# Loading K of one head pair and V of the pair before it with one transfer of rows twice as long

## The chip, the cores and the metric

The kernel runs on one core of one Trainium2 chip. The metric is the device time of one execution in microseconds (us). The kernel before took 520.97 us (median of 4 runs, 520.58 to 522.02).

## The reference

One token passes through two identical layers: attention over the last 4,096 positions of a key and value cache, 32 heads of 192, then a gated MLP. There is one query, so each K and V element is used once per layer and the work is moving data. wq and wo are the weights that make the query and that turn the heads' outputs into the result.

```python
def _A_ref(x, k_cache, v_cache, wq, wo):          # D = 640, Hq = Hkv = 32, Dh = 192, W = 4096
    q = (x @ wq).reshape(...)                     # [1, 32, 1, 192]
    k = k_cache[:, :, Sk - W:, :]; v = v_cache[:, :, Sk - W:, :]
    p = softmax(einsum("bhqd,bhkd->bhqk", q, k) * Dh ** -0.5)
    return einsum("bhqk,bhkd->bhqd", p, v).reshape(...) @ wo
x = x + _A_ref(layernorm(x), ...); x = x + _B_ref(layernorm(x), ...)   # MLP, F = 1536
x = x + _A_ref(layernorm(x), ...); x = x + _B_ref(layernorm(x), ...)   # the same weights and caches again
```

## The kernel before

Heads go in 16 pairs. A pair has two units of 14,208 bf16 elements per partition: an A unit (wq and K) and a B unit (V and wo). On-chip memory holds seven slots of one unit and an area for the MLP weights. Every unit is one transfer of 128 rows of 28,416 B, from two arrays in memory. A slot is loaded again when its last reader is done. What fits is kept for layer 1 (pairs 0, 14, 15 and K of pair 1).

```python
def slot(s, o, n):
    return big[:, s * UNIT + o:s * UNIT + o + n]
A_SLOT = [{p: p % 2 for p in range(NPAIR)}, {p: 5 if p % 2 else 2 for p in range(NPAIR)}]
B_SLOT = [{p: 2 + p % 2 for p in range(NPAIR)}, {p: 3 if p % 2 else 6 for p in range(NPAIR)}]
# ... exceptions at the ends cut
# order of loads: a0, a1, b0, a2, b1, a3, b2, ...; the last V of a layer in three pieces (b1, b0, b0)
if k in ("a", "b"):
    s = (A_SLOT if k == "a" else B_SLOT)[it[1]][it[2]]
    if not take(s):
        return False                              # its slot is still in use
    pg.dma(q_dma(slot(s, 0, n), (ua if k == "a" else ub)[it[2]][:, 0:n]), f"s{s}", wr=[rslot[s]])

def step(p, prev):                                # one pair; p's scores, prev's values
    if l == 0 and prev > 0:
        PVn(prev - 1, 1 - prev % 2)               # times wo; releases the B slot of prev - 1
    Q(p, 0); QK(p, 0)                             # query, scores; releases the A slot of p
    soft(); expo()
    PVmm(prev, prev % 2)                          # weights times V
    ET(p % 2); PVt(prev % 2)
    if l == 1:
        PVn(prev, prev % 2)
```

`PVn`, the product with wo, is the last reader of a B slot.

## Time and profile before

The first view is the page of the kernel before, cut to the engines' busy times (PE is the matrix engine, PEld its weight loads, DVE VectorE, ACT ScalarE, POOL GpSimd), the 40 equal slices of the span with the DMA engines' busy tenths and their GB/s, and the table of DMA queues.

```profile
span 520.6 us, 8422 instructions
PE 272.0 (52%) x3716; PEld 139.7 (27%) x3716; DVE 98.0 (19%) x372; ACT 87.6 (17%) x171; POOL 2.0 (0%) x5
...
DMA  8999999999999999999999999999999999999996
GB/s 352 427 439 427 433 430 430 432 430 430 434 430 429 432 434 426 437 430 425 430 414 382 371 437 434 429 427 436 429 424 439 430 426 434 432 424 434 423 424 273
DMA packets 11835, 219.45 MB, mean 422 GB/s; under 512 B 1448, under 2 KB 1448, under 8 KB 4264
...
q1 hardware_dynamic: 11672, 219.13, 98.9%
q8 instruction: 13, 0.21, 0.2%
```

The queue of loads keeps the 16 DMA engines busy for 98.9% of the span, while the matrix engine is busy for 52%. The rate is flat at about 430 GB/s but for the start, the end and three slices at the layer boundary (382 and 371 among them).

The waits view of the same kernel (engine, tile and line, who released it: us in total, times, longest) shows the matrix engine waiting for both kinds of load.

```profile
PE bank L351 <- DMA big<-in_ua_dram: 71.1, 22, 4.1
...
PE o L420 <- DMA big<-in_ub_dram: 52.3, 26, 2.5
```

The timeline shows one pair in the steady loop (start us, us, engine, line and operation, and in brackets the idle time before it and what ended that; SPq is the queue that issues the loads).

```profile
140.78 0.56 PE L351 MATMUL bank<-sh,big 128*128 128x1 bf16 x15 [3.10 <-DMA big<-in_ua_dram]
141.69 2.75 PE L366 MATMUL scores<-big,qs 128*32 128x512 bf16 x24 [0.35 <-DVE qs L354]
144.48 0.33 SPq L182 DMA_DIRECT2D big<-in_ua_dram  x1
...
149.20 2.73 PE L420 MATMUL o<-big,et_sb 128*2 128x384 bf16 x32 [2.20 <-DMA big<-in_ub_dram]
...
153.99 0.56 PE L450 MATMUL bank<-sh,big 128*128 128x1 bf16 x15 [0.55 <-DVE sh L439]
154.58 0.33 SPq L182 DMA_DIRECT2D big<-in_ub_dram  x1
```

K lands (140.78), the scores are made, K's slot is loaded again (144.48); V lands (149.20), wo is applied, V's slot is loaded again (154.58). These loads land about 30 us after their issue, so in the steady loop about two and a half loads are queued ahead of each:

```profile
big<-in_ua_dram SPq DMA_DIRECT2D x27, 3552.0 KB, 30.0
big<-in_ub_dram SPq DMA_DIRECT2D x24, 3552.0 KB, 28.3
```

(That is the list of DMA issues: what, how many, KB each, median us from issue to landing.) The trace also has a record for each row that an engine moved. Their median durations, of the kernel before:

```
row, bytes   3,840   7,680   15,360   16,384   24,576   28,416
median, ns     149     292      575      611      912     1,055
```

### The profile page before, as it was taken

Reading aid. Unit: us, or ns where it says so; the run is one execution under the profiler, and the core shown is the slowest. Engines: PE = TensorE matmul, PEld = TensorE weight load, DVE = VectorE, ACT = ScalarE, POOL = GpSimd, SP = SyncE. Lnnn points to the kernel's source line nnn. Section 1 sums busy time; section 2 is a strip of 40 time slices with the busy share of each in tenths; the row PEclk is TensorE's granted clock in tenths of the full one; section 3 lists DMA queues with packets and bytes.
Section 4 is the critical chain, followed back from the end, with each engine's and each line's share of the span. In section 5 each row is a group of like instructions: output and inputs, shape, how many; then the busy total and the mean of one; then the engine's idle time right before and its main releaser. Section 6 shows DMA issues by size and latency. Waiting matters only on the chain. (4 is left out here: it accounts for less than half of the span.)

```text
span 520.6 us, 8422 instructions
## 1 busy us (share of the span) xinstructions
PE 272.0 (52%) x3716; PEld 139.7 (27%) x3716; DVE 98.0 (19%) x372; ACT 87.6 (17%) x171; POOL 2.0 (0%) x5
## 2 busy tenths in 40 slices
PE   0645354545445453645465667866354545455465
PEld 0322122212222222222224434433122212222234
DVE  0222111111111201211121233322111211121211
ACT  0112102210121112210120023132102211121110
POOL 0010000000000000000000000000000000000000
PEclk9999766556555555555565559776555555556655
DMA  8999999999999999999999999999999999999996
GB/s 352 427 439 427 433 430 430 432 430 430 434 430 429 432 434 426 437 430 425 430 414 382 371 437 434 429 427 436 429 424 439 430 426 434 432 424 434 423 424 273
DMA packets 11835, 219.45 MB, mean 422 GB/s; under 512 B 1448, under 2 KB 1448, under 8 KB 4264
## 3 DMA queue, kind: packets, MB, share of 16 engines
q1 hardware_dynamic: 11672, 219.13, 98.9%
q8 instruction: 13, 0.21, 0.2%
q10 hardware_dynamic: 144, 0.06, 0.0%
q14 instruction: 6, 0.05, 0.0%
HBM read 219.18 MB, written 0.00 MB: 421 GB/s over the span
## 5 line engine op out<-in xcount | busy, mean ns | idle before, releaser
L420 PE MATMUL o<-big,et_sb 128*2 128x384 bf16 x1024 | 81.7, 488 | 52.3 <-DMA big<-in_ub_dram 52.3
L366 PE MATMUL scores<-big,qs 128*32 128x512 bf16 x744 | 82.5, 611 | 9.9 <-DVE qs L354 9.8
L379 ACT ACTIVATE diag<-cst,sc 128x128 f32<-128x128 bf16 x32 | 12.8, 401 | 265.7 <-DVE sc L376 258.8
L351 PE MATMUL bank<-sh,big 128*128 128x1 bf16 x480 | 17.5, 166 | 72.0 <-DMA big<-in_ua_dram 71.1
L376 DVE TENSOR_REDUCE sc<-scores 128x1 f32<-128x1024 f32 x31 | 38.0, 1224 | 80.3 <-PE scores L366 80.3
L420 PEld LDWEIGHTS o<-big,et_sb 128*2 128x2 bf16 x1024 | 28.0, 109 | 92.9 <-DMA big<-in_ub_dram 60.9
L382 PE MATMUL bank<-diag,sc 128*128 128x128 f32 x64 | 23.3, 463 | 48.4 <-ACT diag L379 48.4
L390 ACT ACTIVATE e_sb<-scores,sc 128x1024 bf16<-128x1024 f32 x31 | 37.3, 1205 | 41.7 <-DVE sc L385 39.8
L425 ACT CAST o_sb<-o 128x384 bf16<-128x384 f32 x64 | 30.3, 477 | 70.7 <-PE o L420 70.6
L351 PEld LDWEIGHTS bank<-sh,big 128*128 128x128 bf16 x480 | 15.7, 105 | 74.9 <-DMA big<-in_ua_dram 72.9
L366 PEld LDWEIGHTS scores<-big,qs 128*32 128x32 bf16 x744 | 23.9, 132 | 44.0 <-issue 30.7
L382 PEld LDWEIGHTS bank<-diag,sc 128*128 128x128 f32 x64 | 14.6, 285 | 73.8 <-ACT diag L379 72.3
L400 DVE CAST et_sb<-bank 128x64 bf16<-128x64 f32 x32 | 7.2, 225 | 122.4 <-PE bank L396 122.4
L354 DVE TENSOR_TENSOR qs<-bank,cst 128x96 bf16<-128x96 f32 x32 | 8.2, 258 | 103.5 <-PE bank L351 103.2
L450 PE MATMUL bank<-sh,big 128*128 128x1 bf16 x480 | 17.6, 166 | 15.8 <-DVE sh L439 15.6
L403 PE MATMUL bank<-sc 128*128 128x2 f32 x64 | 16.5, 328 | 14.5 <-DVE sc L401 14.5
L450 PEld LDWEIGHTS bank<-sh,big 128*128 128x128 bf16 x480 | 14.9, 102 | 18.3 <-DVE sh L439 17.3
L403 PEld LDWEIGHTS bank<-sc 128*128 128x128 f32 x64 | 13.8, 268 | 17.3 <-DVE sc L401 17.3
L383 DVE TENSOR_REDUCE sc<-bank 128x2 f32<-128x128 f32 x32 | 9.3, 292 | 42.3 <-PE bank L382 42.3
L396 PEld LDWEIGHTS bank<-cst,e_sb 128*128 128x128 bf16 x256 | 9.1, 104 | 22.9 <-ACT o_sb L425 16.5
L396 PE MATMUL bank<-cst,e_sb 128*128 128x8 bf16 x256 | 11.9, 170 | 5.6 <-ACT e_sb L390 5.6
L405 DVE RECIPROCAL sc<-bank 64x1 f32<-64x1 f32 x64 | 10.6, 166 | 20.5 <-PE bank L403 19.5
(61 smaller groups left out, 101.3 us busy)
## 6 DMA issues: line engine op xcount, KB each, us to landing
big<-in_ua_dram SPq DMA_DIRECT2D x27, 3552.0 KB, 30.0
big<-in_ub_dram SPq DMA_DIRECT2D x24, 3552.0 KB, 28.3
big<-in_ub_dram SPq DMA_DIRECT2D x2, 3072.0 KB, 27.0
big<-in_ub_dram SPq DMA_DIRECT2D x4, 768.0 KB, 17.4
big<-in_wd_dram SPq DMA_DIRECT2D x3, 960.0 KB, 7.6
big<-in_ua_dram SPq DMA_DIRECT2D x1, 2048.0 KB, 13.1
big<-in_ub_dram SPq DMA_DIRECT2D x1, 2016.0 KB, 16.3
big<-in_ub_dram SPq DMA_DIRECT2D x4, 480.0 KB, 18.0
```

Of the source, the lines that this page charges most:

```text
L351: ins = t.matmul(qe[:, i:i + 1], lhsT=slot(sa, c * 2 * DH + c0, P), rhs=xq[:, c:c + 1], start=(c == 0), stop=(c == DC - 1))
L366: ins = t.matmul(sc_x[1 + b][32 * j:32 * j + 32, :], lhsT=qs[:, y, k, :], rhs=slot(sa, WQE + k * W + (4 * b + j) * 512, 512), start=(k == ...
L376: pg.op("dve", lambda v: v.reduce_max(out=mx, in_=sc_x[0][:], axis=AX.X), wr=[res("mx")], ex=sc_x[3:5])
L379: pg.op("act", lambda a: a.mul(out=diag[:], in_=ident, mul=mx), rd=[res("cst"), res("mx")], wr=[res("diag")])
L382: pg.op("pe", lambda t: t.matmul(dmx[:, 0:P], lhsT=ones_f, rhs=diag[:], start=True, stop=True), rd=[res("diag"), res("ones")], ex=[rb[2]])
L390: pg.op("act", lambda a: a.activation(out=e_sb[:], in_=sc_x[0][:], func=ACT.Exp, bias=nbias, scale=srs_c, accum_out=rowsum), rd=[res("nbia ...
L396: ins = t.matmul(qe[:, 0:2 * NB].rearrange("p (r x) -> p r x", r=2)[:, :, 4 * b:4 * b + 4], lhsT=e_sb[:, b * P:(b + 1) * P], rhs=sel, star ...
L403: pg.op("pe", lambda t: t.matmul(dmx[:, P:P + 2], lhsT=ones_f, rhs=rs2, start=True, stop=True), rd=[res("rs2"), res("ones")], ex=[rb[2]])
L405: pg.op("dve", lambda v, h=h: v.reciprocal(out=Rn[z][64 * h:64 * h + 64], in_=dmx[64 * h:64 * h + 64, P + h:P + h + 1]), wr=[res(f"Rn{z}{h ...
L420: ins = t.matmul(o8[h][32 * j:32 * j + 2, 0:2 * DH].rearrange("p (a d) -> p a d", a=2), lhsT=et_sb[:, z, h * NB + 2 * u:h * NB + 2 * u + 2 ...
L425: pg.op("act", lambda a, h=h: a.copy(out=o8_sb[:, :, h * DH:(h + 1) * DH], in_=o8[h][:, 0:2 * DH].rearrange("p (a d) -> p a d", a=2)), wr= ...
L450: ins = t.matmul(yT[:, j:j + 1], lhsT=wo[:, c * D + j * P:c * D + (j + 1) * P], rhs=oTb[z][:, c:c + 1], start=False, stop=(c == 2), skip_g ...
```

## The change

The intent is fewer and longer rows. In memory, the A unit of pair p now lies beside the B unit of pair p - 1, and so do their slots on chip (which of the two comes first alternates with p). A new item "c" loads both with one transfer of 128 rows of 56,832 B. The two slots are filled together, and only when both are free. V's arrival is passed on through a one-element GpSimd memset, so that the matrix engine can wait for one count whether V came jointly or alone. The loads around the layer boundary and at the end of layer 1 stay separate, and so do K of pair 6 and V of pair 5 in layer 1. V and wo of pair 0, two loads before, come with the first joint one, and GpSimd's copy of that wo now runs early.

```diff
+    PLACE = {s: i for i, s in enumerate((0, 3, 2, 1, 4, 5, 6))}
     def slot(s, o, n):
-        return big[:, s * UNIT + o:s * UNIT + o + n]
+        return big[:, PLACE[s] * UNIT + o:PLACE[s] * UNIT + o + n]
...
-    A_SLOT = [{p: p % 2 for p in range(NPAIR)}, {p: 5 if p % 2 else 2 for p in range(NPAIR)}]
-    B_SLOT = [{p: 2 + p % 2 for p in range(NPAIR)}, {p: 3 if p % 2 else 6 for p in range(NPAIR)}]
+    A_SLOT = [{p: p % 2 for p in range(NPAIR)}, {p: 6 if p % 2 else 3 for p in range(NPAIR)}]
+    B_SLOT = [{p: 2 + p % 2 for p in range(NPAIR)}, {p: 2 if p % 2 else 5 for p in range(NPAIR)}]
...
+    seq = [("a", 0, 0)] + [("c", 0, p) for p in range(1, 15)] + [("a", 0, 15), ("b", 0, 14)] + last_values(0, 15)
+    seq += [("wol", 14), ("wol", 15)] + [(k,) for k in (*MW, *MV)] + [("wom",), ("a0", 0), ("a0", 1), ("a", 1, 3), ("b", 1, 2)]
+    seq += [("c", 1, p) for p in range(4, 13)] + [("a", 1, 13), ("b", 1, 12)] + last_values(1, 13)
     seq += [("fg",), ("fu",), ("fd", 0), ("fd", 1), ("fd", 2)]
+    seq = [y for x in seq for y in ([("a", *x[1:]), ("b", x[1], x[2] - 1)] if x in (('c', 1, 6),) else [x])]
...
+    def values_in(s):
+        pg.op("pool", lambda g: g.memset(tick, 0.0), rd=[rslot[s], res("tick")], wr=[rval[s], res("tick")])
...
+        if k == "c":
+            l, p = it[1:]
+            ss = A_SLOT[l][p], B_SLOT[l][p - 1]
+            if any(x in busy for x in ss):
+                return False
+            busy.update(ss)
+            first = min(ss, key=PLACE.get)
+            pg.dma(q_dma(slot(first, 0, 2 * UNIT), uc[p]), f"c{l}{p % 2}", wr=[rslot[x] for x in ss])
+            values_in(ss[1])
```

More of the change, by code (lines that the diff above doesn't have):

```diff
@@ L105, in decode_kernel @@
 @with_exitstack
-def decode_kernel(ctx: ExitStack, nc, cx: bass.AP, ua: bass.AP, ub: bass.AP,
+def decode_kernel(ctx: ExitStack, nc, cx: bass.AP, uc: bass.AP,
                   wg_d: bass.AP, wu_d: bass.AP, wd_d: bass.AP, out: bass.AP):
@@ L125, in decode_kernel @@
     et_sb = sb("et_sb", [P, 2, 2 * NB], BF16)
-    sc = sb("sc", [P, 24 + 5 * DC + 2 * FC], FP32)
+    sc = sb("sc", [P, 25 + 5 * DC + 2 * FC], FP32)
+    tick = sc[0:1, 24 + 5 * DC + 2 * FC:25 + 5 * DC + 2 * FC]
     mx, nbias, rowsum, rs_c, ss_c, lnv_c, srs_c, rstd_c, eps_a, eps_m, ones_c, Rn_0, Rn_1 = (sc[:, i:i + 1] for i in range(13))
@@ L166, in decode_kernel @@
     rslot = [res(f"slot{i}") for i in range(NSLOT)]
+    rval = [res(f"val{i}") for i in range(NSLOT)]
     rc = [res(f"cell{i}") for i in range(-(-ME // FW))]
@@ L171, in decode_kernel, with v_at, wo_at, a_in @@
     VAFTER = {"v0": "up2", "v1": "up1", "v2": "down0", "v3": "down1"}
+    PLACE = {s: i for i, s in enumerate((0, 3, 2, 1, 4, 5, 6))}
     def slot(s, o, n):
-        return big[:, s * UNIT + o:s * UNIT + o + n]
+        return big[:, PLACE[s] * UNIT + o:PLACE[s] * UNIT + o + n]
+    def v_at(p):
+        return 0 if p % 2 else WOE
+    def wo_at(p):
+        return VE if p % 2 else 0
+    def a_in(p, o0=0, o1=UNIT):
+        o = UNIT if p % 2 else 0
+        return uc[p][:, o + o0:o + o1]
+    def b_in(p, o0=0, o1=UNIT):
+        o = UNIT if p % 2 else 0
+        return uc[p + 1][:, o + o0:o + o1]
     def mreg(o, n):
@@ L193, in decode_kernel, with last_values @@
     NHALF = NB * DH // 2
-    def stream(l, ps):
-        q = list(ps)
-        out_ = []
-        for i, p in enumerate(q):
-            out_.append(("a", l, p))
-            if i:
-                out_.append(("b", l, q[i - 1]))
-        return out_ + [("b1", l, q[-1]), ("b0", l, q[-1], 0), ("b0", l, q[-1], 1)]
-    seq = stream(0, range(NPAIR))
-    seq.insert(seq.index(("b", 0, 0)) + 1, ("wo0",))
-    seq += [("wol", 14), ("wol", 15)] + [(k,) for k in (*MW, *MV)]
-    tail = stream(1, range(2, 14))
-    assert tail[0] == ("a", 1, 2)
-    seq += [("wom",), ("a0", 0), ("a0", 1)] + tail[1:]
+    def last_values(l, p):
+        return [("b1", l, p), ("b0", l, p, 0), ("b0", l, p, 1)]
+    seq = [("a", 0, 0)] + [("c", 0, p) for p in range(1, 15)] + [("a", 0, 15), ("b", 0, 14)] + last_values(0, 15)
+    seq += [("wol", 14), ("wol", 15)] + [(k,) for k in (*MW, *MV)] + [("wom",), ("a0", 0), ("a0", 1), ("a", 1, 3), ("b", 1, 2)]
+    seq += [("c", 1, p) for p in range(4, 13)] + [("a", 1, 13), ("b", 1, 12)] + last_values(1, 13)
     seq += [("fg",), ("fu",), ("fd", 0), ("fd", 1), ("fd", 2)]
+    seq = [y for x in seq for y in ([("a", *x[1:]), ("b", x[1], x[2] - 1)] if x in (('c', 1, 6),) else [x])]
     seq_pos = [0]
-    busy = {2}
+    busy = set()
     ev_done = {}
@@ L223, in take @@
         return True
+    def values_in(s):
+        pg.op("pool", lambda g: g.memset(tick, 0.0), rd=[rslot[s], res("tick")], wr=[rval[s], res("tick")])
     def try_load(it):
         k = it[0]
-        if k in ("a", "b"):
-            s = (A_SLOT if k == "a" else B_SLOT)[it[1]][it[2]]
+        if k == "c":
[5 more added lines that the diff above has]
+            first = min(ss, key=PLACE.get)
+            assert abs(PLACE[ss[0]] - PLACE[ss[1]]) == 1 and first == ss[p % 2]
+            pg.dma(q_dma(slot(first, 0, 2 * UNIT), uc[p]), f"c{l}{p % 2}", wr=[rslot[x] for x in ss])
+            values_in(ss[1])
+        elif k == "a":
+            s = A_SLOT[it[1]][it[2]]
             if not take(s):
                 return False
-            n, n0 = VE if it in (("b", 0, 0), ("b", 0, 14)) else UNIT, len(pg.ops["dma"])
-            pg.dma(q_dma(slot(s, 0, n), (ua if k == "a" else ub)[it[2]][:, 0:n]), f"s{s}", wr=[rslot[s]])
-            if it == ("b", 0, 14):
+            pg.dma(q_dma(slot(s, 0, UNIT), a_in(it[2])), f"a{it[1]}_{it[2]}" if (it[1], it[2]) in ((0, 0), (1, 3)) else f"c{it[1]}{it[2] % 2}", wr=[rslot[s]])
+        elif k == "b":
+            s = B_SLOT[it[1]][it[2]]
+            if not take(s):
+                return False
+            o0, n0 = WOE if it[1:] == (0, 14) else 0, len(pg.ops["dma"])
+            pg.dma(q_dma(slot(s, o0, UNIT - o0), b_in(it[2], o0)), f"b{it[1]}_{it[2]}", wr=[rslot[s]])
+            if it[1:] == (0, 14):
                 ev_done["b14"] = list(pg.ops["dma"][n0]["deps"].items())
+            values_in(s)
         elif k == "b1":
@@ L239, in try_load @@
             n, o1 = len(pg.ops["dma"]), UNIT if it[1] else VE
-            pg.dma(q_dma(slot(s, NB * DH, o1 - NB * DH), ub[it[2]][:, NB * DH:o1]), f"s{s}", wr=[rslot[s]])
+            pg.dma(q_dma(slot(s, NB * DH, o1 - NB * DH), b_in(it[2], NB * DH, o1)), f"b1_{it[1]}", wr=[rslot[s]])
             ev_done["b1"] = list(pg.ops["dma"][n]["deps"].items())
@@ L244, in try_load @@
             o = it[3] * NHALF
-            pg.dma(q_dma(slot(s, o, NHALF), ub[it[2]][:, o:o + NHALF]), f"bh{it[3]}", wr=[res(f"bh{it[3]}")], extra=ev_done["b1"])
+            pg.dma(q_dma(slot(s, o, NHALF), b_in(it[2], o, o + NHALF)), f"bh{it[3]}", wr=[res(f"bh{it[3]}")], extra=ev_done["b1"])
         elif k == "a0":
@@ L250, in try_load @@
             o0, o1 = ((0, A0CUT), (A0CUT, UNIT))[it[1]]
-            pg.dma(q_dma(slot(s, o0, o1 - o0), ua[2][:, o0:o1]), f"a0{it[1]}", wr=[res(f"a0{it[1]}")] + ([rslot[s]] if it[1] else []),
+            pg.dma(q_dma(slot(s, o0, o1 - o0), a_in(2, o0, o1)), f"a0{it[1]}", wr=[res(f"a0{it[1]}")] + ([rslot[s]] if it[1] else []),
                    extra=[ev_done[f"a14_{it[1]}"]])
-        elif k == "wo0":
-            s = B_SLOT[0][2]
-            pg.dma(q_dma(slot(s, VE, WOE), ub[0][:, VE:UNIT]), f"s{s}", wr=[rslot[s]])
         elif k == "wol":
             s = B_SLOT[0][it[1]]
-            pg.dma(q_dma(slot(s, VE, WOE), ub[it[1]][:, VE:UNIT]), f"wol{it[1]}", wr=[res(f"wol{it[1]}")], extra=ev_done["b1" if it[1] == 15 else "b14"])
+            o = wo_at(it[1])
+            pg.dma(q_dma(slot(s, o, WOE), b_in(it[1], o, o + WOE)), f"wol{it[1]}", wr=[res(f"wol{it[1]}")], extra=ev_done["b1" if it[1] == 15 else "b14"])
         elif k in MW:
@@ L269, in try_load @@
             o0, o1 = c0 * FW, min(c1 * FW, ME)
-            pg.dma(q_dma(mreg(o0, o1 - o0), ub[PM][:, o0:o1]), k, wr=rc[c0:c1])
+            pg.dma(q_dma(mreg(o0, o1 - o0), b_in(PM, o0, o1)), k, wr=rc[c0:c1])
         elif k == "wom":
@@ L273, in try_load @@
                 return False
-            pg.dma(q_dma(slot(A_SLOT[1][PM], 0, WOE), ub[PM][:, VE:UNIT]), "wom", wr=[res("wom")], extra=[ev_done["QM"]])
+            pg.dma(q_dma(slot(A_SLOT[1][PM], 0, WOE), b_in(PM, VE, UNIT)), "wom", wr=[res("wom")], extra=[ev_done["QM"]])
         elif k == "fg":
@@ L300, in decode_kernel @@
     pg.dma(q_dma(cst[:, 0:CE], cx), "x", wr=[res("cst")], q="adma")
+    while seq_pos[0] < 2:
+        assert try_load(seq[seq_pos[0]])
+        seq_pos[0] += 1
+    pg.op("pool", lambda g: g.tensor_copy(out=slot(2, wo_at(0), WOE), in_=slot(5, wo_at(0), WOE)), rd=[rslot[5]], wr=[rslot[2]])
+    busy.add(2)
     prefetch()
@@ L412, in PVmm @@
             for h in (1, 0) if half else (0, 1):
-                vt = (mreg(h * NB * DH, NB * DH) if inm else slot(sv, h * NB * DH, NB * DH)).rearrange("p (t d) -> p t d", t=NB)
+                vt = (mreg(h * NB * DH, NB * DH) if inm else slot(sv, v_at(p) + h * NB * DH, NB * DH)).rearrange("p (t d) -> p t d", t=NB)
                 for part in (0, 1) if half and h == 0 else (None,):
@@ L422, in f @@
                         return ins
-                    rV = rc if inm else [rslot[sv]] + ([] if part is None else [res(f"bh{part}")])
-                    pg.op("pe", f, rd=[res(f"et{z}")] + rV, ex=[rb[4 + h]])
+                    rV = rc if inm else [rslot[sv]] + ([] if part is None else [res(f"bh{part}")]) if half else [rval[sv]]
+                    ev = pg.op("pe", f, rd=[res(f"et{z}")] + rV, ex=[rb[4 + h]])
+                    if not inm and not half:
+                        rslot[sv].rd.append(ev)
                 pg.op("act", lambda a, h=h: a.copy(out=o8_sb[:, :, h * DH:(h + 1) * DH], in_=o8[h][:, 0:2 * DH].rearrange("p (a d) -> p a d", a=2)),
@@ L444, in PVn @@
             sv = None if inm else 2 if l == 0 and p == 0 else B_SLOT[l][p]
-            wo = slot(A_SLOT[1][PM], 0, WOE) if inm else slot(sv, VE, WOE)
+            wo = slot(A_SLOT[1][PM], 0, WOE) if inm else slot(sv, wo_at(p), WOE)
             def im(t):
@@ L453, in PVn @@
             sa = A_SLOT[1][PM]
-            pg.op("pe", im, rd=[res(f"oTb{z}")] + ([res("wom"), rslot[sa]] if inm else [rslot[sv]]) + ([res(f"wol{p}")] if p > 13 or (l == 1 and p == 0) else []), ex=[rb[7]])
+            if inm:
+                rw = [res("wom"), rslot[sa]]
+            elif l == 0 and p == 0:
+                rw = [rslot[2]]
+            elif p in (14, 15):
+                rw = [rslot[sv], res(f"wol{p}")]
+            else:
+                rw = [rslot[sv] if (l, p) in halves else rval[sv]]
+            ev = pg.op("pe", im, rd=[res(f"oTb{z}")] + rw, ex=[rb[7]])
+            if not inm and not (l == 0 and p == 0):
+                rslot[sv].rd.append(ev)
             if inm:
                 release(sa)
+            elif l == 0 and p == 0:
+                release(2)
             elif not (l == 0 and ("b", p) in KEPT):
                 release(sv)
-            if l == 0 and p == 0:
-                pg.op("pool", lambda g: g.tensor_copy(out=slot(5, VE, WOE), in_=slot(2, VE, WOE)), rd=[rslot[2]], wr=[res("wol0")])
-                release(2)
         def scale_pm():
@@ L770, in _layout @@
     v = vc[0, :, SK - W:].reshape(NPAIR, 2, 2, 4, 4, P, DH)
-    ua = np.empty((NPAIR, P, UNIT), bf)
-    ub = np.empty((NPAIR, P, UNIT), bf)
+    uc = np.zeros((NPAIR + 1, P, 2 * UNIT), bf)
     q = wq.reshape(DC, P, NPAIR, 2, DH)
-    qv = ua[:, :, :WQE].reshape(NPAIR, P, DC, 2 * DH)
-    for h in range(2):
-        qv[..., h * P:(h + 1) * P] = q[:, :, :, h, :P].transpose(2, 1, 0, 3)
-        qv[..., 2 * P + h * 64:2 * P + (h + 1) * 64] = q[:, :, :, h, P:].transpose(2, 1, 0, 3)
-        ua[:, :, WQE + h * W:WQE + (h + 1) * W] = k[:, h, :, :P].transpose(0, 2, 1)
-        ua[:, h * 64:(h + 1) * 64, WQE + 2 * W:] = k[:, h, :, P:].transpose(0, 2, 1)
-    ua[:, :, :WQE] = qv.reshape(NPAIR, P, WQE)
-    ub[:, :, :VE] = v.transpose(0, 5, 1, 2, 4, 3, 6).reshape(NPAIR, P, VE)
-    ub[:, :, VE:] = wo.reshape(NPAIR, P, WOE)
+    for n in range(NPAIR):
+        a = uc[n][:, n % 2 * UNIT:(n % 2 + 1) * UNIT]
+        b = uc[n + 1][:, n % 2 * UNIT:(n % 2 + 1) * UNIT]
+        qv = a[:, :WQE].reshape(P, DC, 2 * DH)
+        for h in range(2):
+            qv[..., h * P:(h + 1) * P] = q[:, :, n, h, :P].transpose(1, 0, 2)
+            qv[..., 2 * P + h * 64:2 * P + (h + 1) * 64] = q[:, :, n, h, P:].transpose(1, 0, 2)
+            a[:, WQE + h * W:WQE + (h + 1) * W] = k[n, h, :, :P].T
+            a[h * 64:(h + 1) * 64, WQE + 2 * W:] = k[n, h, :, P:].T
+        a[:, :WQE] = qv.reshape(P, WQE)
+        vo, wf = (0, VE) if n % 2 else (WOE, 0)
+        b[:, vo:vo + VE] = v[n].transpose(4, 0, 1, 3, 2, 5).reshape(P, VE)
+        b[:, wf:wf + WOE] = wo[n * 2 * DH:(n + 1) * 2 * DH].reshape(P, WOE)
     blk = lambda w: np.ascontiguousarray(w.reshape(DC, P, FC, P).transpose(1, 2, 0, 3).reshape(P, FC * FW))
@@ L801, in _layout @@
     cx[:, C_X:] = x.reshape(DC, P).T
-    return dict(cx=cx, ua=ua, ub=ub, wg=blk(wg), wu=blk(wu), wd=wdn)
+    return dict(cx=cx, uc=uc, wg=blk(wg), wu=blk(wu), wd=wdn)
 def kernel(**inputs):
```

## The prediction

> **What bounds it now.** The DMA queue. The page's queue table puts 98.9% of the span of 16 engines on the SP queue (219.1 MB); the 40 slices show 425 to 439 GB/s in all but the first, the last and three around the layer boundary. The matrix engine is busy 52%. In the steady stretches (windows of 17 us) the DMA share is 1.00 to 1.01, and 3.64 MB loads land 8.436 us apart, with 20 to 22 us of queued work ahead at each issue. About 3 us of stall sit at the layer boundary, where small loads wait for the MLP, 2 us at the start, 2.5 us after the last landing.
>
> **What the change does.** It puts a pair's K (with wq) beside the previous pair's V (with wo), in memory and on chip, and loads both with one transfer: rows of 56,832 B instead of two of 28,416 B, 22 times, and a 23rd merge where V and wo of pair 0 were two loads. Bytes and tensor work are unchanged.
>
> **What that is worth.** In the trace's DMA records a row's time is linear in its size: 3,840 B 149 ns, 16,384 B 611 ns, 24,576 B 912 ns, 28,416 B 1,053 to 1,055 ns. The slope is about 27.2 B/ns, the intercept 8 to 10 ns. The slope agrees with the Trainium skill, "DMA: Bandwidth & Descriptors", section "Where 436 GB/s comes from" (16 ports x 32 B x 850 MHz = 435 GB/s, 27.2 per engine). So the queue already runs at 99% of that ceiling and only the fixed part of a row can go. Estimate from the records: each engine moves 8 rows per load and writes one semaphore (9 ns): 8 x 8.7 + 9 = 78 ns per merge, 23 merges = 1.8 us. All of it lies on the critical path.
>
> **What it costs.** A pair's two slots are now freed and filled together, so K waits for V. From K's landing to the release of the previous pair's V slot takes about 11.6 us in the steady loop (14 us now, less 2.2 us of waiting for V). The next transfer lands 16.8 us after, and a transfer's first data needs about 1.1 us from issue, its first rows slow (1.5 to 2.8 us). So the queue's reserve at an issue falls from 20-22 us to about 5 us but not to zero. At the start pair 1 lands at about 30 us instead of 21: matrix engine idle, not the queue. At the layer boundary and the end the matrix chain starts one half-pair (about 8 us) later but has waits to absorb it; I compute 0 to 0.5 us. The GpSimd ticks (24 memsets) delay nothing on the path.
>
> **Prediction.** 519.3 us, range 518.2 to 521.2; faster by over 2%: 0.01, within 2%: 0.96, slower by over 2%: 0.03.
>
> **What would show each step.** Rows of 56,832 B at 2,095 to 2,100 ns in the DMA records; landings of merged loads 16.79 us apart instead of 16.87; about 2,800 fewer packets; reserve at issue near 5 us; waits of the matrix engine for K longer (from about 3 to about 5 us), waits for V gone; the span after the last landing still 2.5 us; boundary stalls still about 3 us.
>
> **What would make it wrong.** If the hardware cuts a 56,832 B row back into pieces, the gain is nil (about 521). If the reserve runs out somewhere, each time costs up to about 2 us. If half-row loads out of the wider array read HBM more slowly or long rows delay instruction fetches, the saving could be lost.

## The result and the profile after

The changed kernel took 520.22 us (median of 9 runs, 518.76 to 521.51) beside 520.78 us for the kernel before. The ratio is 0.9985, with a 95% interval of 0.997 to 1.0. A ratio here is the mean time of one kernel's fast runs over that of the other's of the same rounds, so it is not quite the ratio of the quoted medians. That job alone left open whether the gain was nothing or nearly the whole 1.8 us. Two more jobs gave 519.27 us (ratio 0.9974, 0.995 to 0.9997) and 519.01 us (ratio 0.9972, 0.9957 to 0.9987).

The two profiles first compared flatter the change. The kernel before was profiled in a run of 521.92 us, above its median, and the changed one in a run of 519.35 us, below its median. Their spans differ by 2.6 us, the medians by 0.6 us. Where time went is therefore read from intervals, not from the spans.

The same parts of the page after:

```profile
span 518.0 us, 8458 instructions
PE 262.5 (51%) x3716; PEld 135.2 (26%) x3716; DVE 97.9 (19%) x372; ACT 85.0 (16%) x171; POOL 4.2 (1%) x31
...
DMA packets 8524, 219.46 MB, mean 424 GB/s; under 512 B 1080, under 2 KB 1080, under 8 KB 3768
...
q1 hardware_dynamic: 8360, 219.12, 98.8%
q8 instruction: 13, 0.21, 0.2%
```

The page counts each row and each semaphore write as a packet. The same bytes go in 3,312 fewer packets on the queue of loads: 22 x 128 rows and 128 more for wo of pair 0, and 368 semaphore writes (23 transfers fewer, 16 each). One more instruction fetch makes it 3,311 on the whole. The rows of 56,832 B are one record each, with a median of 2,099 ns, the shortest 2,095 ns.

The waits view after:

```profile
PE bank L383 <- DMA big<-in_uc_dram: 123.8, 21, 12.2
...
PE o L452 <- DMA big<-in_uc_dram: 3.6, 4, 1.4
```

One pair on the timeline after, with GpSimd's memset (its first line merges two issues, at 142.49 and 159.21 us):

```profile
142.49 17.04 SPq L200 DMA_DIRECT2D big<-in_uc_dram  x2
147.62 0.56 PE L383 MATMUL bank<-sh,big 128*128 128x1 bf16 x15 [5.21 <-DMA big<-in_uc_dram]
147.68 0.09 POOL L236 MEMSET sc<- 1x1 f32 x1 [16.69 <-DMA big<-in_uc_dram]
148.54 2.75 PE L398 MATMUL scores<-big,qs 128*32 128x512 bf16 x24 [0.35 <-DVE qs L386]
...
153.78 2.73 PE L452 MATMUL o<-big,et_sb 128*2 128x384 bf16 x32
158.57 0.56 PE L484 MATMUL bank<-sh,big 128*128 128x1 bf16 x15 [0.55 <-DVE sh L473]
```

The wait for V is gone (none stands before 153.78), and the wait for K grew from 3.10 to 5.21 us. The matrix engine only traded one wait for another, off the critical path. What the trade costs is the depth of the queue:

```profile
big<-in_uc_dram SPq DMA_DIRECT2D x22, 7104.0 KB, 22.4
```

A joint load takes 16.8 us to move and lands 22.4 us after its issue, so about 5.6 us of work is queued ahead of it. Below, this is called the **reserve**: the time from a load's issue to the landing of the load before it. It has two values, since the 16 engines do not finish together. On the engine that lands last it was 5.1 to 6.5 us at most issues of joint loads; on the engine that lands first it was 3.3 to 4.7 us in layer 0, and down to 1.8 us in layer 1.

The next table cuts the runs' profiles at loads that all the kernels have. It is worked out from the times at which the last engine reports a load: from the first load (K of pair 0) to V of pair 14; to the wo of pair 15, across the three pieces of V of pair 15; to K of pair 2 of layer 1, across the MLP; and to the last MLP weights. Each row is one profiled run; the kernels of experiments 5, 7, 8 and 11 are left out (251.9 to 252.3, 9.86 to 9.88, 32.8 to 34.0 and 207.5 to 209.0 us).

```
kernel (run)            ->V14    ->wo15  ->K2, layer 1  ->end
before                  253.50    9.85      34.07       207.98
before (again)          253.49    9.83      34.55       208.02
changed                 252.05    9.85      33.88       207.64
changed (again)         252.95   11.06      33.83       208.14
changed (third)         252.29    9.87      33.30       207.64
short rows              253.38    9.87      32.87       209.55
V of pair 15 held back  252.15   10.48      32.90       208.28
two loads taken apart   252.44    9.87      32.68       208.42
the same, again         252.01    9.87      32.63       207.84
```

Three things stand out. The first column falls by 0.5 to 1.5 us with the long rows; their fixed cost predicts 1.17 us there (15 merges x 78 ns). The second column is the same everywhere but in two runs, one of which was made so on purpose. The third column varies by almost 2 us with no visible relation to rows (quarter rows, below, has 32.34 us with the schedule of the kernel before).

### The profile page after: what moved, and what is told of

The parts are those of the page before. It is cut to its first block, busy times and chain, and to the rows that moved or that the text cites. A ratio compares the mean times of both kernels' runs of the same rounds, so it can differ in the third digit from the quotient of the medians.

```text
span 518.0 us, 8458 instructions
## 1 busy us (share of the span) xinstructions
PE 262.5 (51%) x3716; PEld 135.2 (26%) x3716; DVE 97.9 (19%) x372; ACT 85.0 (16%) x171; POOL 4.2 (1%) x31
## 4 chain that ended last, share of the span: by engine, by line
DMA 62%; PE 24%; DVE 8%; ACT 2%; issue 2%; SPq 1%; POOL 0%; ACTq 0%; POOLq 0%; DVEq 0%
DMA big<-in_uc_dram 53%; PE scores L398 8%; PE o L452 7%; DMA big<-in_wd_dram 6%; DMA big<-in_wu_dram 3%; DVE sc L408 3%; PE bank L414 2%; PE bank L435 2%; PE bank L383 2%; PE bank L484 1%; SPq L200 1%; ACT e_sb L422 1%; PE bank L428 1%; ACT diag L411 1%; DVE sc L437 1%
## 5 line engine op out<-in xcount | busy, mean ns | idle before, releaser
L398 PE MATMUL scores<-big,qs 128*32 128x512 bf16 x744 | 83.6, 618 | 9.9 <-DVE qs L386 9.8
L383 PE MATMUL bank<-sh,big 128*128 128x1 bf16 x480 | 17.5, 166 | 124.6 <-DMA big<-in_uc_dram 123.8
L452 PE MATMUL o<-big,et_sb 128*2 128x384 bf16 x1024 | 77.3, 467 | 5.2 <-DMA big<-in_uc_dram 3.6
L414 PE MATMUL bank<-diag,sc 128*128 128x128 f32 x64 | 22.4, 446 | 48.0 <-ACT diag L411 47.9
L435 PE MATMUL bank<-sc 128*128 128x2 f32 x64 | 14.3, 293 | 14.5 <-DVE sc L433 14.5
L435 PEld LDWEIGHTS bank<-sc 128*128 128x128 f32 x64 | 11.5, 225 | 17.4 <-DVE sc L433 17.4
## 6 DMA issues: line engine op xcount, KB each, us to landing
big<-in_uc_dram SPq DMA_DIRECT2D x22, 7104.0 KB, 22.4
big<-in_uc_dram SPq DMA_DIRECT2D x1, 2016.0 KB, 10.3
```

The lines of the kernel that those rows point to most:

```text
L383: ins = t.matmul(qe[:, i:i + 1], lhsT=slot(sa, c * 2 * DH + c0, P), rhs=xq[:, c:c + 1], start=(c == 0), stop=(c == DC - 1))
L398: ins = t.matmul(sc_x[1 + b][32 * j:32 * j + 32, :], lhsT=qs[:, y, k, :], rhs=slot(sa, WQE + k * W + (4 * b + j) * 512, 512), start=(k == ...
L414: pg.op("pe", lambda t: t.matmul(dmx[:, 0:P], lhsT=ones_f, rhs=diag[:], start=True, stop=True), rd=[res("diag"), res("ones")], ex=[rb[2]])
L435: pg.op("pe", lambda t: t.matmul(dmx[:, P:P + 2], lhsT=ones_f, rhs=rs2, start=True, stop=True), rd=[res("rs2"), res("ones")], ex=[rb[2]])
L452: ins = t.matmul(o8[h][32 * j:32 * j + 2, 0:2 * DH].rearrange("p (a d) -> p a d", a=2), lhsT=et_sb[:, z, h * NB + 2 * u:h * NB + 2 * u + 2 ...
```

## The experiments

Twelve experiments ran, in four jobs (1 to 4, 5 to 8, 9 to 11, and 12), each job on another chip. All gave correct results. The job of experiments 5 to 8 and that of experiment 12 held the kernel before but not the changed kernel.

**1. The changed kernel again**, no edit.

> The changed kernel again, for a tighter mean and a second profile. Theory A (the whole gain is the fixed cost of the removed rows, 23 merges x 78 ns, and nothing gives it back; the first 0.8 us was scatter): 1.8 us below the kernel before, ratio about 0.9966, and landings of merged loads 16.79 us apart. Theory B (the thinner reserve of queued transfers gives part of it back in many runs): again about 0.8 us, ratio about 0.9985, and a scatter of runs wider than that of the kernel before.

It took 519.27 us (median of 6 runs, 518.56 to 521.79), ratio 0.9974, between the two theories. Four runs were at 519.53 us or below and two above 521.4 us. Its profile is of one of the slow two (521.79 us); joint loads land 16.79 us apart there too.

**2. The kernel before against itself.**

> The kernel before against itself: ratio 1.000; what it shows beyond that is noise. A second profile of it, to see which stalls at the layer boundary repeat: if they are scatter, the gaps of 1.07 us (second down-projection load) and 0.79 us (third V piece) seen in the first profile move elsewhere or vanish.

It took 520.25 us (5 runs), ratio 0.9991 (0.9971 to 1.0012). So 0.1% is noise in one job. The stall of the second down-projection load, 1.07 us in the first profile, was gone on the last engine (2.31 us for a load that takes 2.34), but the first down-projection load now came 1.1 us late and the third V piece 0.9 us late. In these two profiles the stalls belong to the place, not to a particular load.

**3. Joint transfers with short rows.** The waits, slots and order of the changed kernel, but the two halves of a row lie apart in memory:

```diff
-    uc = np.zeros((NPAIR + 1, P, 2 * UNIT), bf)
+    uc = np.zeros((NPAIR + 1, 2, P, UNIT), bf)
...
-    pg.dma(q_dma(slot(first, 0, 2 * UNIT), uc[p]), ...)
+    pg.dma(q_dma(slot(first, 0, 2 * UNIT).rearrange("p (a u) -> p a u", a=2), uc[p].rearrange("a p u -> p a u")), ...)
```

> The changed kernel with its 22 joint transfers, slots and waits, but each row of 56,832 B kept as two rows of 28,416 B (the two halves lie apart in memory). Theory A: all of the gain of the rows is lost except 22 semaphore writes of 9 ns (0.2 us): landings of joint loads about 16.86 us apart, time 1.5 us above the changed kernel, within 0.5 us of the kernel before. Theory B: the same row cost, but the schedule's loss is now bare: 0.8 us or more above the kernel before.

It took 520.49 us (5 runs, 519.91 to 521.94), ratio 0.9991 (0.9971 to 1.0011), level with the kernel before, as the row theory has it. The times alone do not decide (the interval reaches down to a gain of 0.3%); the landings do. Joint loads landed 16.86 to 16.87 us apart, against 16.79 us with long rows. The windows view of the stretch from 80 to 245 us (length; busy us of each engine, in the order of the page; the matrix engine's granted clock; DMA share; GB/s) shows it, for the kernel before, the changed kernel and this one, in this order:

```profile
80.00:245.00 165.00, 82.33 (x1034) 39.89 (x1038) 26.98 (x98) 26.15 (x49) 0.00 (x0) 0.53 1.00 431
```

```profile
80.00:245.00 165.00, 78.05 (x1040) 38.51 (x1040) 28.58 (x100) 25.13 (x50) 0.88 (x10) 0.58 1.00 434
```

```profile
80.00:245.00 165.00, 76.06 (x1040) 37.53 (x1040) 28.59 (x100) 25.03 (x50) 0.88 (x10) 0.61 1.00 430
```

The DMA share is 1.00 in all three; only the long rows move more per microsecond. The joint schedule alone brings nothing that these runs show. It can also lose: the profile of this kernel has one load (K of pair 4 with V of pair 3) that landed 1.3 us late (18.18 us), issued with a reserve of 0.2 us on the first engine and 2.9 us on the last.

**4. Quarter rows.** The kernel before, its 51 full loads cut into rows of 7,104 B:

```diff
...
+    src = (ua4 if k == "a" else ub4)[it[2]].rearrange("r p u -> p r u")      # [4, 128, UNIT / 4] in memory
+    pg.dma(q_dma(slot(s, 0, n).rearrange("p (r u) -> p r u", r=4), src), f"s{s}", wr=[rslot[s]])
```

> The kernel before with nothing changed but its 51 full loads cut into rows of 7,104 B instead of 28,416 B (3 more rows per partition, no more semaphores, same waits). If a row costs a fixed 8.7 ns whatever its size: 51 x 8 x 3 x 8.7 ns = 10.6 us more, about 531.5 us, ratio about 1.020, full loads landing 8.65 us apart instead of 8.44. If the records' intercept is no cost of the queue (rows overlap), no change: ratio 1.000.

It took 532.05 us (5 runs, 531.67 to 532.77), ratio 1.0217 (1.0196 to 1.0238). Full loads landed 8.66 us apart instead of 8.435, which is 0.225 us for 24 more rows per engine, or 9.4 ns a row. The joint loads give the same: 16.865 - 16.79 us for 8 rows is also 9.4 ns. The same window:

```profile
80.00:245.00 165.00, 79.93 (x1001) 38.89 (x1001) 27.10 (x98) 26.12 (x49) 0.00 (x0) 0.53 1.01 420
```

The packets more than doubled, the engines stayed full, and the rate fell to 420 GB/s. A row's fixed cost is real time of a full queue.

**5. One joint load taken apart.** The slow profile of experiment 1 had a stall of 1.2 us at the first load of V of pair 15 (the 11.06 us in the table above). That load needs the slot of V of pair 13. In the kernel before it was issued at 255.8 us with 10.3 us of reserve on the last engine; in the changed kernel the step of pair 14 starts half a pair later, and it is issued at 259.6 to 260.5 us with 4.4 to 4.5 us on the last engine and 1.9 to 2.7 us on the first. Here K of pair 14 and V of pair 13 come separately again:

```diff
-    ... if x in (('c', 1, 6),) else [x])]
+    ... if x in (('c', 1, 6), ('c', 0, 14)) else [x])]
```

> The changed kernel with one joint transfer (K of pair 14 with V of pair 13, the last before the layer boundary) taken apart again. Theory C (the runs near 521.5 us are those in which the queue runs dry before the first load of V of pair 15, which is issued only when pair 13's slot is free, 1.9 to 2.7 us before the fastest engine's queue ends): that load is issued some 4 us earlier, no stall there in the profile (first and last landing 3.70 us after the load before), the runs near 521.5 us go, median about 519.2 us though one merge (78 ns) is given up. Theory A (scatter only): 0.08 us slower than the changed kernel and the same two groups of runs.

It took 519.06 us (6 runs, 518.40 to 520.62), ratio 0.9971 (0.9955 to 0.9988). The load was issued at 253.9 us with 8.3 us of reserve on the first engine, and landed 3.69 to 3.71 us after the one before, on first and last engine. One run in six was still at 520.62 us, so the expectation held but for that run. The changed kernel did not run in that job, so it is not shown that this one is faster.

**6. The same load held back on purpose**, until the scores of pair 15 are done:

```diff
+            if l == 0 and p == 15:
+                mark("QK15", ev)
...
-    pg.dma(..., f"b1_{it[1]}", wr=[rslot[s]])
+    pg.dma(..., f"b1_{it[1]}", wr=[rslot[s]], extra=[] if it[1] else [ev_done["QK15"]])
```

> The changed kernel with the same load held back on purpose, until the scores of pair 15 are done (about 3.8 us later than now, or 4.4 us). Theory C: each microsecond of an empty queue there is lost: 2 to 3 us slower than the changed kernel, about 522 us, all runs in one group. If the layer boundary has slack to take it up (the weights behind it wait for the MLP anyway): under 0.5 us slower.

It took 521.27 us (5 runs, 519.61 to 521.81), ratio 1.0012 (0.9997 to 1.0027), against 0.9971 for experiment 5 in the same job: 2.2 us between the medians. The profiled run is the fastest of the five. In it the load was issued at 262.20 us with 0.04 us of reserve on the first engine and 1.85 us on the last, and landed 1.8 us late on the first and 0.6 us late on the last. The windows view from 262 to 271 us, of the changed kernel (third run), of its slow run (experiment 1), and of this kernel:

```profile
262.00:271.00 9.00, 6.14 (x83) 2.54 (x74) 2.60 (x9) 3.02 (x6) 0.09 (x1) 0.68 0.98 408
```

```profile
262.00:271.00 9.00, 6.79 (x78) 2.96 (x70) 2.61 (x9) 2.55 (x5) 0.09 (x1) 0.50 0.97 360
```

```profile
262.00:271.00 9.00, 4.42 (x78) 2.07 (x74) 2.60 (x9) 2.92 (x6) 0.09 (x1) 0.88 0.88 344
```

Less is moved there in the last two: 360 and 344 GB/s where 408 are normal. In the held-back kernel the queue runs dry (share 0.88), and 16 of the load's 128 rows, as many as there are engines, took over 600 ns instead of 465. In the slow run the busy share is still 0.97, because rows that were under way took longer (27 over 600 ns, one of 12,288 B 2,779 ns); the two other profiles of the changed kernel, with nearly the same reserve on the last engine (4.5 and 4.4 us), had 2 and 0 such rows. So the slow run's loss is not simply an empty queue.

By the medians the boundary does not take the holding back up: 521.27 us is close to the 522 us expected. Where the slow runs lost it is not seen, since the profiled one made up for its 0.6 us later (32.90 us to K of pair 2, against 33.30 to 33.88 us in the changed kernel). A late V of pair 15 also delays the matrix engine, on which the MLP's weights wait; no run separates that from the empty queue.

**7. The exception in layer 1 removed**: K of pair 6 and V of pair 5 jointly as well.

```diff
-    seq = [y for x in seq for y in ([("a", *x[1:]), ("b", x[1], x[2] - 1)] if x in (('c', 1, 6),) else [x])]
```

> The changed kernel without its one exception in layer 1: K of pair 6 and V of pair 5 also in one transfer. The slots are free when pair 3's output is added, at about 354.4 us, with 3.8 us queued behind the slowest engine and 0.4 us behind the fastest. Row theory alone: 0.08 us faster. Theory C (a queue that runs dry restarts slowly): the fast engines lose 1.5 to 3 us; 0 to 1.5 us slower than the changed kernel depending on how far the slowest engine lags.

It took 519.97 us (6 runs, 519.02 to 522.34), ratio 0.9992 (0.9972 to 1.0013), which is inside the scatter. In the profile the load was issued at 354.36 us with 0.9 us of reserve on the first engine and 4.2 us on the last. The first engine lost 1.1 us (17.86 us between landings), the last none (16.79 us). The matrix engine waits for all 16 engines, and the last one lost nothing, so this stall cost nothing in that run.

**8. Slots released earlier.** The product with V moves from after the exponential to between the scores and the maximum's broadcast, and wo is applied at once (the lines that remove the later `PVn` and shorten the loop are cut):

```diff
...
-            soft()
-            expo()
-            PVmm(prev, prev % 2)
-            ET(p % 2)
+            soft(0, mid=lambda: PVmm(prev, prev % 2))
             PVt(prev % 2)
-            if l == 1:
+            if not (l == 0 and prev == 14):
                 PVn(prev, prev % 2)
+            expo()
+            ET(p % 2)
```

> The changed kernel with V times the weights moved from after the exponential to before it (into the time of the row maximum, where the matrix engine waits), and a pair's output added at once, so that slots come free about 2.5 to 3 us earlier after a landing. Theory C: reserve at each issue of a joint load about 8 us instead of 5 us, no stall at the first load of V of pair 15, median 518.8 to 519.4 us and no runs near 521.5 us: it beats both kernels. Theory A: same as the changed kernel within 0.3 us.

It took 519.50 us (6 runs, 518.12 to 520.94), ratio 0.9979 (0.996 to 0.9998). The reserve rose to 8.5 to 9.3 us on the last engine in the steady loop of layer 1, and the V load of pair 15 did not stall. The joint load of K of pair 4 with V of pair 3 lost 0.7 us (17.47 us), with a reserve of 1.3 us on the first engine and 3.2 on the last. It does not wait for the loop but for the kept pairs 14 and 15 at the start of layer 1. The runs above 520.5 us did not go, so the expectation failed in that.

**9. The changed kernel a third time**, in the job of experiments 10 and 11.

> The changed kernel a third time, beside the two repairs. Theory C: runs from about 518.6 to 521.8 us again, mean near 520.0 us; the queue loses up to 1.3 us, in some runs and not in others, at two loads of the layer boundary: the first V load of pair 15 and the joint load of K of pair 4 with V of pair 3, both issued with under 3 us queued on the fastest engine.

It took 519.01 us (5 runs, 518.92 to 519.18), ratio 0.9972 (0.9957 to 0.9987). The expected scatter did not come, and its profile has no stall at either load, with 2.4 to 2.6 us of reserve on the first engine. So the short reserve does not lose time each time, and a whole job, on one chip, can be free of it.

**10. Both loads at the boundary taken apart**: experiment 5, and V of pair 3 and K of pair 4 each issued when its own slot is free:

```diff
+    ... [("b", 1, 3), ("a", 1, 4)] if x == ("c", 1, 4) else ...
```

> The changed kernel with the two joint loads at the layer boundary taken apart: K of pair 14 and V of pair 13 as in the earlier run, and V of pair 3 and K of pair 4 each issued as soon as its own slot is free. Theory C: over 8 us queued at the V load of pair 3 and at the K load of pair 4, no load in the profile that lands over 0.3 us late at either place, mean about 519.1 us and a narrower range than the changed kernel (two merges, 0.16 us, are given up). If the scatter has another cause: mean about 520.1 us, same range.

It took 519.08 us (5 runs, 518.94 to 519.34), ratio 0.9971 (0.9956 to 0.9986), level with experiment 9. The reserve at the two loads was 12.4 and 15.6 us on the last engine. V of pair 3 landed 0.7 us late on the last engine alone (9.17 us, 8.43 on the first), so against the expectation one load was late; the queue was full, so an empty queue did not cause that. An instruction fetch stands in that load's time (see what stays open, below).

**11. Earlier release, with the load of pairs 3 and 4 taken apart.**

> The kernel with the earlier release of slots, and the joint load of K of pair 4 and V of pair 3 taken apart. Theory C: reserve on the fastest engine above 5 us at every load but those that wait for the MLP, mean about 519.1 us, 0.5 us below the earlier run with the release alone (519.66 us), which lost 0.7 us at that load in its profile. If the scatter has another cause: 519.7 us.

It took 519.46 us (6 runs, 518.56 to 520.63), ratio 0.9985 (0.9966 to 1.0003). No load lost 0.3 us to an empty queue outside the MLP in the profile, and the runs still spread over 2 us. The mean, 519.55 us, is not the 519.1 us expected.

**12. Experiment 10 in a second job**, no further edit.

> The kernel with both joint loads at the layer boundary taken apart, in a second job, since the changed kernel itself was narrow (518.92 to 519.18 us) in the job it was first compared in. If the empty queue at those two loads makes the changed kernel's runs near 521.5 us: all runs again from 518.8 to 519.6 us, mean near 519.1 us. If the scatter belongs to the job and not to those loads: runs above 520.5 us appear here too.

It took 518.80 us (6 runs, 518.35 to 519.28) beside 521.04 us for the kernel before, ratio 0.9961 (0.9947 to 0.9976). No run above 520.5 us appeared, as the first theory has it.

Taken together, the changed kernel had 20 timed runs in three jobs, mean 519.80 us, 7 of them above 520 us; experiment 10's kernel had 11 in two jobs, mean 518.96 us, none above 519.34 us. It beats the kernel before, and it was level with the changed kernel in the one job that held both. So that it is better than the changed kernel is likely, not shown.

## Why the prediction was right or wrong

- **The bound, right.** The DMA queue sets the time before and after. The matrix engine's waits were rearranged (71.1 and 52.3 us for K and V before, 123.8 and 3.6 after) and experiment 3 shows no gain from that by itself. The granted clock is no rival for the gain: the changed kernel's runs had 0.62 to 0.65, mostly more than the kernel before, but the kernel of experiment 3 had 0.63 to 0.66 without the gain.
- **The worth of a row, right, and shown.** The prediction read 8.7 ns of fixed cost from the intercept of the records. The landings gave 9.4 ns, by taking rows away and by adding them (experiments 3 and 4). Rows of 56,832 B took 2,099 ns, at the upper edge of the predicted 2,095 to 2,100, and joint loads landed 16.79 us apart, as predicted. The ceiling agrees too: the Trainium skill, "DMA: Bandwidth & Descriptors", section "Where 436 GB/s comes from", has 435.2 GB/s for 16 ports, an estimated 27.2 GB/s per engine; the slope of the records is 27.1 B/ns (28,416 - 3,840 B in 1,055 - 149 ns), and a joint load (7.27 MB in 16.79 us) ran at 433 GB/s.
- **The time, inside its range.** 520.22 us was measured where 519.3 us was predicted. The range, 518.2 to 521.2 us, also holds the time of the kernel before (520.78 us), so that the time lies in it says little; the row times and landings say more. The predicted gain was 1.7 us; the three jobs gave 0.6, 1.6 and 1.5 us between the medians. Over the three jobs, 20 runs of the changed kernel average 519.80 us and 32 of the kernel before 520.79 us, a gain of 1.0 us with a standard error of 0.3 us, if runs of different jobs count alike. The removed rows are worth 1.8 us by the landings (22 x 0.08 + 0.06 for the merge in pair 0), so in the mean some of it is probably given back.
- **The reserve, the step that was mis-sized.** "... the queue's reserve at an issue falls from 20-22 us to about 5 us but not to zero" holds for the last engine (5.1 to 6.5 us). That figure takes the last engine's landing as the queue's end. In the changed kernel's profiles the engines land up to 3.6 us apart, and on the first one 1.8 to 4.7 us were left. It also gave no account of the two loads at the layer boundary that must wait for slots freed by a later step. There the reserve on the first engine was 0.2 to 3.2 us, and in some profiles 0.7 to 1.3 us was lost on the last engine (experiments 1, 3 and 8). That a load held back until the queue is empty costs time is shown by the medians of experiments 5 and 6. "What would make it wrong" named this case with up to 2 us each time.
- **The boundary, "0 to 0.5 us".** In two of the changed kernel's three profiles the chain across V of pair 15 lost nothing, in one 1.2 us.
- **The smaller points.** The span after the last landing stayed at 2.59 us. The matrix engine's wait for K grew to 5.2 us, as predicted. There are 26 memsets, not 24. The forecast of 2,800 fewer packets (3,311 measured) left out the semaphore writes and the 128 rows of pair 0.

What stays open is the scatter. The last load of the slow run that was profiled (experiment 1) lands 2.5 to 2.9 us after that of the changed kernel's other two profiles. The first load of V of pair 15 gave 1.2 us of that. Two loads that had 6.4 and 7.2 us queued on the last engine gave 0.8 and 0.7 us more, on that engine alone. Taking both boundary loads apart gave 11 runs without a slow one. But the changed kernel also had a job without slow runs, the kernel of experiment 11 spreads although no load but those of the MLP runs short, and the kernel before spreads from 519.6 to 522.8 us with full reserves. The stretch across the MLP, 32.3 to 34.6 us in the profiles of all kernels, is where most of what is left varies. No experiment isolated it. The granted clock does not sort the runs (22 fast runs of the changed kernel: correlation with the time 0.18).

One rival was not looked at: instruction fetches. Each run has 13 or 14 of 16,384 B (q8 on the page, counted on the same 16 engines), most of them about 1 us long in the records. From 80 to 245 us, with the queue never short, the last engine came over 0.2 us late at four loads in the fourteen profiles (by 0.2 to 0.8 us). Each of the four has such a fetch in its time, as at 175.8 us in experiment 1. Four other fetches there made nothing late, and the six profiles without one have no late load. The two full-queue losses above (0.8 and 0.7 us) and the late V of pair 3 in experiment 10 (fetch at 325.9 us) fit this too. That a fetch holds up one engine, and costs time only when that engine is the last, is likely but not shown: the trace does not name the engine.

## What to carry to other kernels

When a kernel already streams at the DMA engines' ceiling, fit row time against row size from the trace: the slope is the ceiling, the intercept times the rows per engine is all that longer rows can win (here 0.35%). Merging transfers also merges the moments at which their buffers come free, so count the reserve at each issue, on the engine that finishes first as well as on the last, and most carefully where the steady loop ends. In these profiles the losses put down to a short reserve came where the first engine had 0.04 to 1.9 us left, and not each time even there (0.9 and 1.8 us cost the last engine nothing); no safe value was measured. When the effect is 0.3%, one pair of profiles can show four times the effect: repeat in several jobs, and compare intervals inside the traces that do not scatter.

## What the Trainium skill lacked or had wrong

- "DMA: Bandwidth & Descriptors", section "Why small descriptors are slow (HBM only)", names a fixed overhead of about 3 cycles per packet. It does not name the clock; at the page's 850 MHz that would be an estimated 3.5 ns. The runs show 9.4 ns per row, at 7,104 B and at 28,416 B alike, so this overhead alone does not account for it; at 7,104 B the added rows cost 2.2% of the time. The section also calls putting consecutive descriptors into one packet worthwhile only at 256 B and less. That is not the same as one longer row, which still gained at 28,416 B.
- "DMA: Bandwidth & Descriptors", section "Rules for kernel authors", asks for 1 MiB or more per transfer and leaves open whether fewer, larger descriptors are faster. Here 3.6 MB transfers in rows of 28,416 B moved 431 GB/s, 7.3 MB in rows of 56,832 B moved 433, and 3.6 MB in rows of 7,104 B moved 420: the row counts, not only the transfer.
- No page that I used says what an empty queue costs. A load issued with 0.04 us queued on the first engine and 1.85 us on the last landed 1.8 us and 0.6 us late (experiment 6, one profile). The first rows of the whole program took 1.5 to 2.8 us in the kernel before, instead of 1.05.
- No page that I used says how far apart the 16 engines finish one load: 0.5 to 3.6 us in these profiles.
